# Queries of the first two batches on 128 partitions: a memory-attention and feed-forward kernel with both of its hand-written opening steps listed anew

## The chip, the cores and the metric

The kernel runs on one core of one Trainium2 chip. The metric is the device time of one execution in microseconds (us); three timed runs of the kernel before gave 669.55, 652.33 and 654.77 us, with a median of 654.77 us.

## What is computed

Eight batches of eight heads, 576 tokens and 64 features go through an attention over 32 memory slots, and the result goes through a feed-forward layer of 512 by 2048. All inputs are float32 in memory, except the two weight matrices, which arrive as 64-bit floats.

```python
a = exp(phi - phi.max(axis=2)); a = a / (a.sum(axis=2) + 1e-09)     # per head: 576 tokens x 32 slots
k_m = einsum('bhsm,bhsd->bhmd', a, k); v_m = einsum('bhsm,bhsd->bhmd', a, v)
scores = q @ k_m.T / sqrt(64)
attn = softmax(scores)                                               # over the 32 slots
x = attn @ v_m                                                       # -> 4608 tokens x 512
out = leaky_relu(x @ w_in, 0.01) @ w_out
```

## The kernel before

The kernel never forms `attn @ v_m`: it multiplies the memory values into `w_in` first ("fold"), so that the transposed attention of a batch (8 heads x 32 slots = 256 rows, in two groups g of 128) meets folded weights. Each float32 product of the feed-forward part is made of three float16 products, except that the first 384 tokens run in float32, while the weights are still being read and their bounds are not yet known. The tokens go in groups G: three groups of 384 (batches 0 and 1), then groups of 256.

A batch b goes through steps named `a<b>.<step>`. `phi`, `k`, `v`, `kv` and `q0`, `q1` load; `A` and `B` make the exponentials of phi; `C1` makes the memory keys and values on TensorE, `C2` and `C30` the reciprocal sums, `C3k` scales the keys (tile `x_k`, ScalarE), `C31` the values (`x_v`, VectorE). `D10` transposes `x_k` on TensorE and `D3` copies the result to `kT`; `D11` and `D5` do that for the values (`vT`). `Q0` and `Q1` turn q in 32x32 blocks on VectorE, `E1` multiplies it with `kT` (the scores, in PSUM tiles `psc`), `E2x` turns the scores back to tokens on partitions, into a tile `t1`. A chunk of tokens c then takes `Sc1` (row maximum, VectorE), `Sc2` (subtract; VectorE in chunk 0 of batch 0, else GpSimd), `Sc3` (exp, ScalarE), `Sc4` (row sums, three VectorE instructions), `Sc5` (multiply), `Sc6` (turn back, into tile `a` or a second buffer `t2`), and, outside chunk 0 of batch 0, `Sc7`, `Sc8` (float16 halves on ScalarE and GpSimd).

The weights come in eight quarters `i0` to `i3` and `o0` to `o3`, each in three pieces: `ld` loads 64-bit words to one of eight slots of a buffer `arena`, `y` and `h` prepare the high and low word (`y` on ScalarE; `h` on ScalarE or VectorE), `t` joins them to float32 on VectorE, `b` sums squares on ScalarE. `f0j.1` folds quarter j on TensorE and `f0j.2` copies it from PSUM on ScalarE. `u0.P0` to `u7.O1` are the eight units of the first token group (`P` up-products, `V` the leaky ReLU, `O` down-products). `z.n` puts n products of a tile of ones on TensorE whose result nobody reads. All float32 products run as two passes on TensorE, so `z.3` is six passes in the trace.

The order on every engine is written out by hand: two lists, `OPENING` and `LATER`, name the steps, and each engine runs its own instructions in that order. SyncE issues every load, in the list's order too; it has eight semaphores for them (`DMAHW0` to `DMAHW7` in the rows below), and each load waits until the one eight loads earlier has landed. PSUM is given out by three pools: `ps_a` (3 banks, tiles `pa`), `ps_h` (2, `ph`) and `ps_o` (3, `po`).

In batches 0 and 1, q lies on 96 partitions: partition p holds tokens 6p to 6p+5 of four heads of one parity. A load has 384 runs of 1536 bytes. The 96 partitions make three token blocks tb of 192 tokens, each a row tile of TensorE's array, and a score product is a 32x32 tile with 192 columns; there are 48 of them for each batch, on twelve tiles. `kT` and `x_k` repeat the keys once for each block. Batches 2 to 7 ("far") go another way, which the change leaves as it is.

Of the kernel before, what the change touches and what calls it, by code (L numbers as in the profile page):

```python
# [44 lines left out]
a0.D4 i1.ld0 o0.h1 u0.V0 o0.y1 u1.P0 u1.P1 o0.h2 u1.V0 o0.t2 i1.ld2 a0.S16 o1.ld2 o1.y0 o1.h0 u0.O0  # L45
o1.ld1 u0.P1 a0.S17 i1.y0 o0.t1 u1.V1 i1.h0 i1.h1 i1.y1 i1.t1 u0.V1 i2.ld0 i1.y2 i1.h2 o1.y1 o1.y2
o1.t0 o1.h1 i1.t0 u1.O0 u0.O1 o1.h2 i2.ld1 o2.ld0 i1.t2 f01.1 i2.h0 i2.y0 i2.y1 a0.S18 i2.h1 i2.t1
i2.ld2 f01.2 o2.ld1 o1.t2 o2.ld2 o1.t1 u1.O1 i2.t0 u2.P1 o2.h0 u2.P0 i2.y2 i2.h2 a1.phi o2.y0 i2.t2
o2.t0 a1.kv1 a1.q0 a1.kv0 f02.1 u2.V0 u3.P1 u2.O0 o2.y1 o2.h1 o2.t1 a1.kv2 o2.y2 o2.h2 a1.kv3 a1.A1
u2.V1 u3.P0 o2.t2 i3.ld0 f02.2 a1.q1 a1.A2 a1.A3 u4.P1 a1.B0 u3.V1 u4.P0 a1.B10 u3.V0 i1.b u3.O0  # L50
i2.b u4.V0 a1.B20 u5.P0 a1.B3 o0.b a1.C10 i3.ld2 a1.Q0 i3.ld1 a1.C2 u5.V0 o1.b u2.O1 i3.y0 u5.P1
u4.V1 a1.C30 a1.C31 a1.C3k a1.C4 a1.D10 a1.D2 o2.b i3.h0 a1.D3 a1.Q1 i3.y2 i3.h2 a1.D11 a1.D4 u3.O1
i3.t2 a1.E1 o3.ld0 a1.D5 i3.y1 u4.O0 i3.h1 i3.t0 o3.h0 u5.V1 o3.y0 o3.ld2 u5.O0 a1.E20 i3.t1 a1.E21
i3.b ci.1 o3.ld1 a1.E22 f03.1 a1.S01 a1.S11 a1.S02 a1.S03 a1.S04 u4.O1 o3.y2 o3.y1 o3.h2 ci.2 o3.t0
f03.2 a1.S12 ci.3 ci.4 e. o3.h1 o3.t1 a1.S05 u6.P0 u6.V0 a1.S13 a1.S06 a1.S07 u6.P1 u7.P0 a1.S14
a1.S15 o3.t2 w0.2 u7.V0 u6.O0 a1.S16 o3.b w1.1 co.1 co.2 u7.O0 w1.2 co.3 u6.V1 co.4 u5.O1 o0.k0
a1.S08 o0.k1 o0.k2 u7.P1 e2. o0.l0 u7.V1 o0.l1 u6.O1 a1.S17 a1.S18 o0.l2 u7.O1
# [125 lines left out]
def kernel(  # L183
# [46 lines left out]
    P = 128  # L230
# [6 lines left out]
    KJ = NG * S // P  # L237
    ND = D // 32
# [270 lines left out]
    def attention(b, steps, chunks, f32_chunks=0):  # L509
# [67 lines left out]
        def load_q(g):  # L577
            if far:
                return load_heads(g)
            t = (ld_slot() if b < FB else at(IO * g, IO))[:CP].rearrange(  # L580
                "p (hh j d) -> p hh j d", hh=HP, j=NJ
            )
            nc.sync.dma_start(
                t, q[b].rearrange("(hh g) (p j) d -> g p hh j d", g=NG, j=NJ)[g]
            )
            ld["q", g] = t
# [143 lines left out]
        def _():  # L730
            x_k = att.tile([P, NG, ND, NB, 32], F32, name="x_k")
            if far:
                both = x_k.rearrange("p g db tb x -> p (g db tb x)")
                var["x_k"], var["kS"] = both[:, 0:P], both[:, P:2 * P]
                for g in range(NG):
                    nc.scalar.activation(
                        var["x_k"][:, g * D:(g + 1) * D], var["pk"][g][:, 0:D], AF.Copy,
                        scale=var["r2"][:, 1, g:g + 1],
                    )
                return  # L740
            var["x_k"] = x_k
            for g in range(NG):
                nc.scalar.activation(
                    x_k[:, g],
                    var["pk"][g][:, 0:D].rearrange("p (db o x) -> p db o x", db=ND, o=1)
                    .broadcast_to([P, ND, NB, 32]),
                    AF.Copy, scale=var["r2"][:, 1, g:g + 1],
                )
# [20 lines left out]
        def _():  # L769
# [4 lines left out]
            var["pkT"] = pkT = ps_a.tile([CP, NG, ND, P], F32, name="pa")  # L774
            for g in range(NG):
                for db in range(ND):
                    nc.tensor.transpose(
                        pkT[:, g, db, :],
                        var["x_k"][:, g, db].rearrange("p tb x -> p (tb x)"), ident,
                    )  # L780
# [14 lines left out]
        else:  # L795
            @step("D3")
            def _():
                var["kT"] = kT = att.tile([CP, NG, ND, P], F32, name="kT")
# [31 lines left out]
        def flip_q(g):  # L830
            if far:
# [9 lines left out]
            flat = (  # L841
                (wi[2], wo[1])[g] if b == 0 else ld["ld", 2 + g] if b == 1
                else at((2 * IO, 0)[g], IO)
            )[:CP, 0:HP * NJ * D]
            nc.vector.transpose(flat, ld["q", g].rearrange("p hh j d -> p (hh j d)"))
            var["qT", g] = flat.rearrange(
                "p (hh j db x) -> p hh j db x", hh=HP, j=NJ, db=ND, x=32
# [19 lines left out]
        def scores(gs_):  # L867
            if "psc" not in var:
                shape = [P, E] if far else [P, NG, SB]
                var["psc"] = [ps_a.tile(shape, F32, name="pa") for tb in range(NB)]  # L870
            psc = var["psc"]
            if far:
                if gs_ == (1,):
                    return rows_by(1, 2, 0, JA, JT)
                rows_by(0, 2, 0, JA, JT)
                for j0 in (0, JA // 2):
                    for hh in range(HP):
                        for g in range(NG):
                            rows_by(g, g, j0 * 32, j0, j0 + JA // 2, (hh,))
                return  # L880
            for g in gs_:
                for db in range(ND):
                    for hh in range(HP):
                        for tb in range(NB):
                            rows = slice(tb * 32, (tb + 1) * 32)
                            cols = slice(hh * M, (hh + 1) * M)
                            nc.tensor.matmul(  # L887
                                psc[tb][cols, g, :], var["kT"][rows, g, db, cols],
                                var["qT", g][rows, hh, :, db, :],
                                start=(db == 0), stop=(db == ND - 1),  # L890
                                tile_position=(tb * 32, hh * M),
                            )

        if b == 0:
            steps[f"{name}E10"] = lambda: scores((0,))
        steps[f"{name}E1"] = lambda: scores((1,) if b == 0 else range(NG))
        if far:
            steps[f"{name}E3"] = lambda: scores((1,))

        def flip(tb):  # L900
            if "t1" not in var:
                var["t1"] = att.tile([P, NB, NG * SB], F32, name="t2", bufs=2)
            if far:
                x0, n = ((0, E), (E, E), (2 * E, D), (2 * E + D, D))[tb]
                flat = var["t1"].rearrange("p tb x -> p (tb x)")
                nc.vector.transpose(flat[:, x0:x0 + n], var["psc"][min(tb, 2)][:, 0:n])
                return
            nc.vector.transpose(
                var["t1"][:, tb], var["psc"][tb].rearrange("p g x -> p (g x)")
            )  # L910

        for tb in range(NB + 1 if far else NB):
            steps[f"{name}E2{tb}"] = lambda tb=tb: flip(tb)


        def chunk(c, b0, b1, f32):
            eng = nc.vector if f32 or b >= FB else nc.gpsimd
            shape = [P, (b1 - b0) * NG * SB // M, M]
# [3 lines left out]
            def t1():  # L922
                flat = var["t1"][:, b0:b1].rearrange("p tb x -> p (tb x)")
# [25 lines left out]
            def s6():  # L949
                if "a" not in st:  # L950
                    st["a"] = att.tile([P, 2 * NG * S], F16, name="a", bufs=2)
                if f32:
                    nc.vector.transpose(
                        a_f32(b)[:, b0:b1].rearrange("p tb x -> p (tb x)"), t1()[0]
                    )
                else:
                    own["t2"] = t2 = att.tile([P, (b1 - b0), NG * SB], F32, name="t2", bufs=2)
                    nc.vector.transpose(t2.rearrange("p tb x -> p (tb x)"), t1()[0])

            def places():  # L960

                t2 = own["t2"].rearrange("p tb (g x) -> p tb g x", g=NG)
                if b < FB:
                    a = a_blocks(b)[:, b0:b1]
                    return a[:, :, 0], a[:, :, 1], t2
                flat, a = own["t2"].rearrange("p tb x -> p (tb x)"), a_columns(b)
# [7 lines left out]
            def piece(x, tb):  # L974
                return x[tb] if b >= FB else x[:, tb]

            def s7():
                hi, lo, t2 = places()
                for tb in range(b1 - b0 if b < FB else 2):
                    nc.scalar.copy(piece(hi, tb), piece(t2, tb))  # L980

            def s8():
                hi, lo, t2 = places()
                for tb in range(b1 - b0 if b < FB else 2):
                    nc.gpsimd.tensor_tensor(  # L985
                        piece(lo, tb), piece(t2, tb), piece(hi, tb), ALU.subtract
                    )
# [5 lines left out]
        for c, (b0, b1) in enumerate(chunks):  # L993
            chunk(c, b0, b1, c < f32_chunks)

    def a_f32(b):

# [487 lines left out]
```

## Time and profile before

| | before |
|---|---|
| timed runs, us | 669.55, 652.33, 654.77 (median 654.77) |
| profiled execution, its own time | 655.37 us |
| span of that execution, first to last instruction | 653.4 us |
| TensorE matmul busy | 635.2 us, 97% of the span |
| VectorE, ScalarE, GpSimd busy | 515.4, 392.5, 29.5 us |
| granted TensorE clock, mean | 0.995 |
| first float32 unit of the feed-forward part (`u0.P0`) starts | 32.68 us |

The profile gives, for each engine, when instructions began and what ended the idle time before them. "Chain" means the page's chain of waits: followed back from the last instruction, at each step to what released it. An engine that is busy all the time sets the length of its stage; a gap on another engine costs nothing by itself. The 2 us between the span and the execution's own time lie outside the instructions.

### The profile page before, as it was taken

The numbers are of one execution on the slowest core, as the hardware profiler recorded it, in microseconds if no ns is written. First come the engines' busy times: TensorE is split into PE (matmuls) and PEld (weight loads), VectorE is DVE, ScalarE is ACT, GpSimd is POOL, SyncE is SP. The second block draws the span as 40 slices with busy tenths as digits, with TensorE's granted clock in tenths as the row PEclk, the third lists the DMA queues.
The fourth block names the chain that finished last, engine by engine and source line by source line (L and its number), as shares of the span: only waits on it lengthen the run. The fifth ranks groups of instructions, "written<-read, shape, count | busy, mean of one in ns | idle before, by whom it ended". The sixth has DMA issues, their size and how long they took to land.

```text
span 653.4 us, 17090 instructions
## 1 busy us (share of the span) xinstructions
PE 635.2 (97%) x7256; PEld 476.3 (73%) x7256; DVE 515.4 (79%) x863; ACT 392.5 (60%) x671; POOL 29.5 (5%) x37
## 2 busy tenths in 40 slices
PE   6799999999999999999999999999999999999997
PEld 3344545665545778888888889887888888889883
DVE  5675889998996899899969975889887897575641
ACT  2698868755473656467546565655665566565543
POOL 0010021000001001001000010000010001000000
PEclk9799999999999999999999999999999999999999
DMA  9999722105601753431155011064104110010102
GB/s 237 405 340 332 246 89 85 46 7 104 194 3 25 142 155 56 111 124 35 25 117 158 1 33 43 11 134 146 34 15 80 27 29 22 14 29 6 34 1 50
DMA packets 85309, 61.16 MB, mean 94 GB/s; under 512 B 61936, under 2 KB 68336, under 8 KB 85232
## 3 DMA queue, kind: packets, MB, share of 16 engines
q1 hardware_dynamic: 85136, 59.94, 33.3%
q8 instruction: 57, 0.93, 0.6%
q10 hardware_dynamic: 96, 0.13, 0.1%
q14 instruction: 20, 0.16, 0.1%
HBM read 50.59 MB, written 9.45 MB: 92 GB/s over the span
## 4 chain that ended last, share of the span: by engine, by line
PE 94%; DMA 2%; ACT 2%; SPq 1%; DVE 0%; issue 0%; ACTq 0%
PE po L1297 31%; PE ph L1229 22%; PE po L1186 16%; PE ph L1114 8%; PE ph L1297 5%; PE pa L1020 4%; PE pa L698 3%; DMA arena<-in_moe_w_in_dram 2%; PE po L1331 1%; PE pa L861 1%; PE pa L1387 1%; ACT wi L1245 1%; PE pa L887 0%; PE pa L344 0%; SPq L549 0%
## 5 line engine op out<-in xcount | busy, mean ns | idle before, releaser
L1297 PEld LDWEIGHTS <-arena 128*128 128x128 f16 x2184 | 209.9, 98 | 31.9 <-issue 8.8
L1245 ACT ACTIVATE wi<-ph,g_sc 128x256 f32<-128x256 f32 (+1 forms) x224 | 99.3, 466 | 164.4 <-PE ph L1229 156.9
L1229 PE MATMUL ph<-a,w_mem 128*128 128x256 f16 (+3 forms) x1440 | 145.3, 246 | 2.9 <-ACT wi L1245 2.9
L1229 PEld LDWEIGHTS <-w_mem 128*128 128x128 f16 x1440 | 114.6, 98 | 17.9 <-issue 6.3
L1297 PE MATMUL po<-arena 128*128 128x256 f16 x936 | 122.2, 273 | 0.0
L1297 PE MATMUL po<-wo,arena 128*128 128x256 f16 x936 | 122.1, 273 | 0.0
L1186 PE MATMUL po<-wo,arena 128*128 128x512 f16 (+1 forms) x384 | 110.3, 433 | 0.0
L1274 DVE TENSOR_TENSOR arena<-arena 128x1024 f16<-128x1024 f32 x52 | 63.6, 1223 | 22.4 <-ACT arena L1270 22.4
L1274 DVE TENSOR_TENSOR arena<-wi,arena 128x768 f16<-128x768 f32 (+1 forms) x60 | 54.7, 912 | 10.1 <-ACT arena L1270 10.1
L1266 DVE TENSOR_TENSOR arena<-wi 128x256 f32<-128x256 f32 x104 | 40.4, 430 | 25.6 <-ACT wi L1245 25.1
L1270 ACT CAST arena<-arena 128x1024 f16<-128x1024 f32 x52 | 54.5, 1047 | 8.2 <-DVE arena L1266 8.0
L1114 PE MATMUL ph<-a,w_mem 128*128 128x192 f16 (+2 forms) x304 | 52.2, 317 | 0.7 <-ACT t L936 0.7
L1186 PEld LDWEIGHTS <-arena 128*128 128x128 f16 x288 | 27.9, 98 | 29.7 <-issue 0.6
L1270 ACT CAST arena<-wi 128x768 f16<-128x768 f32 (+1 forms) x60 | 46.6, 777 | 1.5
L1266 DVE TENSOR_TENSOR arena<-wi,arena 128x256 f32<-128x256 f32 x104 | 45.8, 440 | 1.8
L1297 PE MATMUL ph<-wo,arena 128*128 128x256 f16 x312 | 42.6, 273 | 0.0
L985 POOL TENSOR_TENSOR a<-t,a 128x1024 f16<-128x1024 f32 (+2 forms) x16 | 21.9, 1385 | 431.9 <-ACT a L980 431.9
L1186 PEld LDWEIGHTS po<-wo,arena 128*128 128x128 f32 x96 | 17.7, 190 | 20.3 <-issue 18.5
L1020 PE MATMUL pa<-wi,vT 64*32 64x512 f16 (+1 forms) x704 | 28.9, 420 | 0.4 <-ACT vT L805 0.4
L1114 PEld LDWEIGHTS <-w_mem 128*128 128x128 f16 x240 | 20.7, 98 | 10.3 <-issue 4.1
L1053 ACT ACTIVATE w_mem<-pa 128x512 f16<-128x512 f32 x40 | 22.7, 596 | 8.4 <-PE pa L1020 7.4
L1121 ACT ACTIVATE arena<-ph,g_sc 128x384 f32<-128x384 f32 x32 | 18.4, 581 | 15.6 <-PE ph L1114 15.3
(216 smaller groups left out, 750.9 us busy)
## 6 DMA issues: line engine op xcount, KB each, us to landing
out_dram<-obs SPq DMA_DIRECT2D x142, 64.0 KB, 1.7
arena<-in_k_dram SPq DMA_DIRECT2D x28, 288.0 KB, 4.7
arena<-in_v_dram SPq DMA_DIRECT2D x28, 288.0 KB, 4.9
arena<-in_q_dram SPq DMA_DIRECT2D x96, 72.0 KB, 2.8
arena<-in_moe_w_in_dram SPq DMA_DIRECT2D x12, 512.0 KB, 9.5
arena<-in_moe_w_out_dram SPq DMA_DIRECT2D x8, 768.0 KB, 7.3
arena<-in_phi_dram SPq DMA_DIRECT2D x7, 576.0 KB, 5.1
arena<-in_q_dram SPq DMA_DIRECT2D x4, 576.0 KB, 9.3
```

What stands on the lines that cost most here:

```text
L698: nc.tensor.matmul(var["pk"][g][hh * M:(hh + 1) * M, cs], ld["phi"][rows, hh, j, :], ld["kv", hh][rows, kinds[0]:kinds[-1] + 1, j, :], sta ...
L985: nc.gpsimd.tensor_tensor(piece(lo, tb), piece(t2, tb), piece(hi, tb), ALU.subtract)
L1020: nc.tensor.matmul(pf[g][cols, :], lhs, rhs, start=(n == 0), stop=(n == len(passes) - 1), tile_position=(g * D, hh * M),)
L1053: nc.scalar.activation(tiles(halves(w16(b, j), g)[:, 0]), w(g), AF.Copy, scale=ws)
L1114: nc.tensor.matmul(ph[:, t0:t0 + n * SB], lhs, rhs, start=(m == 0), stop=(m == len(seq) - 1))
L1186: nc.tensor.matmul(po, lhs, rhs, start=(f == 0 and m == 0), stop=(f == NQ * NF - 1 and m == len(seq) - 1),)
L1229: nc.tensor.matmul(ph[:, t0:t0 + n], lhs, rhs, start=(m == 0), stop=(m == len(seq) - 1))
L1245: nc.scalar.activation(dst, ph, AF.Prelu, scale=g_sc2[:, j:j + 1], alpha=SLOPE)
L1266: nc.vector.tensor_tensor(gt[:, x], y, z, op)
L1270: nc.scalar.copy(dst[:, 0], src)
L1274: nc.vector.tensor_tensor(dst[:, 1], src, dst[:, 0], ALU.subtract)
L1297: nc.tensor.matmul(acc, g[:, x, s, u], rhs, start=(h == 0 and j == 0 and u == 0 and m == 0), stop=(j == NQ - 1 and u == 1 and m == 2), ski ...
```

## The change

For batches 0 and 1, a load of q covers two head pairs on all 128 partitions: partition p holds nine tokens of each, in 256 runs of 2304 bytes. A 32-partition block r then holds one head parity g and one block of 288 tokens (r = 2g + block). `x_k` and `kT` repeat the keys twice and not three times; `D10` is two transposes of 128x128 and not four of 128x96. The scores of a batch are 32 products with 288 columns on sixteen 32x32 tiles, in four PSUM tiles and not three. Batch 0 takes these four from three pools (`ph`, `po`, `ph`, `pa`) in one step `E1`; batch 1 takes all from `ps_a`, which has three banks, so blocks 0, 2 and 1 are made in `E1` and block 3 in a step `E3` behind one unit's down-products. The turns back (`E2x`) follow the new blocks; batch 0 has six and batch 1 four, against three each. The chunks of batch 0 stay 384 and 192 tokens; those of batch 1 become 288 and 288 (192 and 384 before). The attention tile `a` is addressed by token columns.

The list `OPENING` is written anew, `LATER` is the same. The diff, cut to its core:

```diff
-a0.phi0 a0.A10 z.4 a0.phi1 a0.A11 a0.A2 a0.k a0.A3 a0.B0 a0.q0 a0.B10 a0.B11 a0.B20 a0.q1 a0.B21
-a0.C10 i0.ld0 i0.ld1 a0.B3 a0.C2 i0.ld2 z.1 a0.C30 a0.v a0.C3k a0.D10 a0.Q0 a0.D3 a0.E10 a0.Q1
-a0.E1 i0.y0 i0.h0 o0.ld0 i0.t0 z.3 a0.E21 a0.E20 i0.y1 i0.h1 o0.ld2 a0.S01 o0.ld1 o1.ld0 i0.y2
-i0.h2 i0.t2 a0.C11 a0.S02 i0.t1 a0.S03 i0.b a0.E22 a0.S11 a0.C31 o0.y0 a0.D11 a0.S12 a0.D5 f00.1
-o0.h0 a0.S04 i1.ld1 o0.y2 a0.S05 f00.2 a0.S06 a0.C4 z.1 a0.S13 u0.P0 a0.D2 o0.t0 a0.S14 a0.S15
+a0.phi0 a0.A10 z.3 a0.phi1 a0.A11 a0.A2 a0.k a0.A3 a0.B0 a0.q0 a0.B10 a0.B11 a0.B20 a0.q1 a0.B21
+a0.C10 i0.ld0 i0.ld1 a0.B3 a0.C2 i0.ld2 z.1 a0.C30 a0.v a0.C3k a0.D10 a0.Q0 a0.D3 a0.Q1 a0.E1 i0.y0
+i0.h0 o0.ld0 i0.t0 z.3 i0.y1 i0.h1 o0.ld2 a0.E20 a0.E21 a0.E22 a0.E23 a0.S01 o0.ld1 o1.ld0 i0.y2
+i0.h2 i0.t2 a0.C11 a0.S02 i0.t1 a0.S03 i0.b a0.E24 a0.E25 a0.S11 a0.S04 a0.C31 o0.y0 a0.D11 a0.S12
+a0.D5 f00.1 o0.h0 i1.ld1 a0.S05 f00.2 a0.S06 a0.C4 z.1 a0.S13 u0.P0 a0.D2 o0.t0 a0.S14 a0.S15
...
-            t = (ld_slot() if b < FB else at(IO * g, IO))[:CP].rearrange(
-                "p (hh j d) -> p hh j d", hh=HP, j=NJ
-            )
+            t = ld["q", g] = ld_slot()[:, 0:2 * KJ * D]
             nc.sync.dma_start(
-                t, q[b].rearrange("(hh g) (p j) d -> g p hh j d", g=NG, j=NJ)[g]
-            )
-            ld["q", g] = t
+                t.rearrange("p (hh j d) -> p hh j d", hh=2, j=KJ),
+                q[b].rearrange("h s d -> (h s) d").rearrange(
+                    "(hh gp j) d -> gp hh j d", gp=P, j=KJ
+                )[:, 2 * g:2 * g + 2],
+            )
...
-            x_k = att.tile([P, NG, ND, NB, 32], F32, name="x_k")
+            x_k = att.tile([P, ND, NG, 2, 32], F32, name="x_k")
...
-            var["pkT"] = pkT = ps_a.tile([CP, NG, ND, P], F32, name="pa")
-            for g in range(NG):
-                for db in range(ND):
...
+            var["pkT"] = pkT = ps_a.tile([P, ND, P], F32, name="pa")
+            for db in range(ND):
+                nc.tensor.transpose(
+                    pkT[:, db, :], var["x_k"][:, db].rearrange("p g tb x -> p (g tb x)"), ident
+                )
...
+        def rows_of(rs):
+
+            for r in rs:
+                pool, name, n = (
+                    (ps_h, "ph", GT), (ps_o, "po", E), (ps_h, "ph", GT), (ps_a, "pa", E)
+                )[r] if b == 0 else (ps_a, "pa", E)
+                psc[r] = pool.tile([P, n], F32, name=name)
+            for x in range(2):
+                for db in range(ND):
+                    for hh in (2 * x, 2 * x + 1):
+                        for r in rs:
+                            rows, cols = slice(r * 32, (r + 1) * 32), slice(hh * M, (hh + 1) * M)
                             nc.tensor.matmul(
-                                psc[tb][cols, g, :], var["kT"][rows, g, db, cols],
-                                var["qT", g][rows, hh, :, db, :],
-                                start=(db == 0), stop=(db == ND - 1),
-                                tile_position=(tb * 32, hh * M),
+                                psc[r][cols, 0:HB], var["kT"][rows, db, cols],
+                                var["qT", x][rows, hh % 2, :, db, :], start=(db == 0),
+                                stop=(db == ND - 1), tile_position=(r * 32, hh * M),
                             )
...
+            steps[f"{name}E1"] = lambda: rows_of((0, 2, 1, 3))
+        else:
+            steps[f"{name}E1"] = lambda: rows_of((0, 2, 1))
+            steps[f"{name}E3"] = lambda: rows_of((3,))
...
-            0: (((0, 2), (2, 3)), 1), 1: (((0, 1), (1, 3)),)
-        }.get(b, (((0, NB),),)))
+            0: (((0, GT), (GT, S)), 1), 1: (((0, HB), (HB, S)),)
+        }.get(b, (((0, S),),)))
```

Three places show what this moves. The first is TensorE in batch 0, from the transposed keys to the first product of the values (`pa`, `ph`, `po` are PSUM tiles, `wi_87` and `wo_91` the two turned halves of q, `ones` the products without use, `wi_88` the exponentials of phi and `wo_92` the values; the brackets name the engine or the load that the row waits for). Before:

```order
L777 MATMUL pa<-ident,x_k 96x128
L887 MATMUL pa<-wi_87,kT 32x192 [waits DVE_49,Activation_49]
L887 MATMUL pa<-wi_87,kT 32x192 [waits PE_49] x2
L887 MATMUL pa<-wi_87,kT 32x192 x21
L887 MATMUL pa<-wo_91,kT 32x192 [waits DVE_49]
L887 MATMUL pa<-wo_91,kT 32x192 x23
L1387 MATMUL pa<-ones 128x512 [waits DVE_49]
L1387 MATMUL pa<-ones 128x512 x2
L698 MATMUL po<-wo_92,wi_88 32x64 [waits DMAHW5_49]
```

And now:

```order
L778 MATMUL pa<-ident,x_k 128x128
L876 MATMUL ph<-wi_87,kT 32x288 [waits DVE_49,Activation_49]
...
L876 MATMUL ph<-wo_91,kT 32x288 [waits DVE_49]
...
L876 MATMUL pa<-wo_91,kT 32x288
L1379 MATMUL pa<-ones 128x512 [waits PE_49]
L1379 MATMUL pa<-ones 128x512 x2
L700 MATMUL po<-wo_92,wi_88 32x64 [waits DMAHW5_49]
```

The products of ones (`z.3`) waited for VectorE, which had to turn one score tile back and so free a bank; now only one of the four score tiles is in that pool, and they wait for nothing but TensorE itself.

The second place is VectorE in batch 0, from the second piece of `i0` to the end of chunk 0 (`t` holds the scores, `tm` and `ts` maxima and sums, `x_v` the values, `a` the finished chunk). Before:

```order
L406 SCALAR_TENSOR_TENSOR wi_86<-arena 128x768 [waits DMAHW3_49,DMAHW2_49]
L908 STREAM_TRANSPOSE t_308<-pa 128x384 [waits PE_49]
L928 TENSOR_REDUCE tm<-t_308 128x12 [waits DVE_49]
L754 TENSOR_SCALAR x_v<-po,r_228 128x64 [waits PE_49] x2
L940 TENSOR_REDUCE ts__420<-t_308 128x24 [waits Activation_49]
L941 TENSOR_SCALAR ts__420<-ts__420 128x24 [waits DVE_49]
L942 RECIPROCAL ts__420<-ts__420 128x24 [waits DVE_49]
L945 TENSOR_TENSOR t_308<-t_308,ts__420 128x768 [waits DVE_49]
L953 STREAM_TRANSPOSE a<-t_308 128x768 [waits DVE_49]
```

And now:

```order
L408 SCALAR_TENSOR_TENSOR wi_86<-arena 128x768 [waits DMAHW3_49,DMAHW2_49]
L921 STREAM_TRANSPOSE t_293<-po 128x192
L921 STREAM_TRANSPOSE t_293<-pa 128x192
L942 TENSOR_REDUCE tm<-t_293 128x12 [waits DVE_49]
L954 TENSOR_REDUCE ts__385<-t_293 128x24 [waits Activation_49]
L955 TENSOR_SCALAR ts__385<-ts__385 128x24 [waits DVE_49]
L956 RECIPROCAL ts__385<-ts__385 128x24 [waits DVE_49]
L756 TENSOR_SCALAR x_v<-po,r_227 128x64 [waits PE_49] x2
L959 TENSOR_TENSOR t_293<-t_293,ts__385 128x768 [waits DVE_49]
L967 STREAM_TRANSPOSE a<-t_293 128x768 [waits DVE_49]
```

The three instructions of the row sums (`S04`) stood behind the scaled values (`C31`), which wait for TensorE; now they stand ahead of them. The turn back of the rest became two instructions.

The third place is TensorE in batch 1, around the scores (`po` rows are down-products of the first token group). Before:

```order
L1186 MATMUL po<-wo_92,arena 128x512 x3
L887 MATMUL pa<-arena,kT 32x192 [waits DVE_49,Activation_49]
L887 MATMUL pa<-arena,kT 32x192 [waits PE_49]
L887 MATMUL pa<-arena,kT 32x192 [waits Activation_49]
L887 MATMUL pa<-arena,kT 32x192 x45
L1186 MATMUL po<-wo_93,arena 128x512 x6
```

And now:

```order
L1189 MATMUL po<-wo_92,arena 128x512 x3
L876 MATMUL pa<-arena,kT 32x288 [waits DVE_49,Activation_49]
L876 MATMUL pa<-arena,kT 32x288 [waits DVE_49]
L876 MATMUL pa<-arena,kT 32x288 [waits Activation_49]
L876 MATMUL pa<-arena,kT 32x288 x21
L1189 MATMUL po<-wo_93,arena 128x512 x3
L876 MATMUL pa<-arena,kT 32x288 [waits DVE_49]
L876 MATMUL pa<-arena,kT 32x288 x7
L1189 MATMUL po<-wo_93,arena 128x512 x3
```

The last eight products wait for VectorE to free a bank, with the three down-products of `u4.O0` ahead of them.

More of the change, by code (lines that the diff above doesn't have):

```diff
@@ L46 @@
[L46 to L56, printed above, removed]
@@ new lines @@
+a1.kv3 u3.P0 o2.t2 i3.ld0 a0.S18 f02.2 a1.q1 a1.A2 a1.A3 u4.P1 a1.B0 u3.V1 u4.P0 a1.B10 u3.V0 i1.b
+u3.O0 i2.b u4.V0 a1.B20 u5.P0 a1.B3 o0.b a1.C10 i3.ld2 i3.ld1 a1.C2 u5.V0 o1.b u2.O1 i3.y0 u5.P1
+u4.V1 a1.C30 a1.C31 a1.C3k a1.C4 a1.D10 a1.Q0 a1.D2 o2.b i3.h0 a1.D3 a1.Q1 i3.y2 i3.h2 a1.D11 i3.t0
+a1.D4 u3.O1 i3.t2 o3.ld0 a1.D5 a1.E1 i3.y1 u4.O0 a1.E3 a1.E20 i3.h1 a1.E21 a1.E22 u5.V1 o3.y0
+o3.ld2 i3.t1 i3.b u5.O0 a1.E23 o3.ld1 f03.1 a1.S01 a1.S11 a1.S02 ci.1 a1.S03 o3.h0 a1.S04 u4.O1
+o3.y2 o3.h2 ci.2 o3.t0 f03.2 a1.S12 ci.3 o3.y1 ci.4 e. o3.h1 a1.S05 u6.P0 u6.V0 a1.S13 a1.S06
@@ L58 @@
+a1.S07 o3.t1 u6.P1 u7.P0 a1.S14 a1.S15 o3.t2 w0.2 u7.V0 u6.O0 a1.S16 o3.b w1.1 co.1 co.2 u7.O0 w1.2
+co.3 u6.V1 co.4 u5.O1 o0.k0 a1.S08 o0.k1 o0.k2 u7.P1 e2. o0.l0 u7.V1 o0.l1 u6.O1 a1.S17 a1.S18
+o0.l2 u7.O1
 """
@@ L237 @@
     KJ = NG * S // P
+    HB = S // NG
     ND = D // 32
@@ L917, in chunk @@
+        def chunk(c, x0, x1, f32):
             eng = nc.vector if f32 or b >= FB else nc.gpsimd
-            shape = [P, (b1 - b0) * NG * SB // M, M]
+            w = NG * (x1 - x0)
+            shape = [P, w // M, M]
             n = f"{name}S{c}"
```

199 lines of the change are left out of this document (87 added, 112 removed).

## Prediction

> **What bounds the kernel now.** I read the page's busy times and slices first, then windows, then the chain of waits through the opening.
>
> ```profile
> span 653.4 us, 17090 instructions
> PE 635.2 (97%) x7256; PEld 476.3 (73%) x7256; DVE 515.4 (79%) x863; ACT 392.5 (60%) x671; POOL 29.5 (5%) x37
> PE   6799999999999999999999999999999999999997
> DMA  9999722105601753431155011064104110010102
> ...
> 40.00:60.00 20.00, 20.00 (x80) 8.81 (x78) 13.61 (x18) 16.63 (x27) 0.00 (x0) 1.00 0.99 328
> 60.00:80.00 20.00, 20.00 (x289) 11.18 (x289) 14.36 (x24) 18.55 (x26) 0.00 (x0) 1.00 0.84 276
> 300.00:650.00 350.00, 347.51 (x4175) 298.59 (x4172) 261.63 (x439) 203.57 (x363) 11.59 (x11) 1.00 0.20 48
> ```
>
> TensorE is busy for all of 40 to 80 us and for 347.5 of the last 350 (the first number behind a window's length is PE). So there are two ways to win: let TensorE's unbroken stretch begin earlier, or take work out of it. Loads fill the DMA engines only in the first eight slices or so. The chain shows what the beginning hangs on:
>
> ```profile
> 5.97 12.91 DMA arena<-in_moe_w_in_dram
> 18.96 0.92 ACT arena L397
> 20.68 0.96 DVE wi L406
> 21.64 0.50 DVE t L908
> 22.19 4.84 PE pa L1387 x6
> 27.03 1.63 PE po L698 x102
> 28.66 0.47 DVE x_v L754 x2
> 29.54 0.27 ACT vT L805
> 31.21 0.95 ACT w_mem L1370 x2
> 32.68 1.53 PE ph L1114 x4
> ```
>
> The first piece of `i0` lands at 18.88; ScalarE and VectorE convert it (`y0`, `h0`, `t0`); behind `t0` VectorE turns a score tile back, which frees a bank for the six useless passes of `z.3`; behind those come the values (`C11`), their scaling, the first fold, and at 32.68 `u0.P0`, from which TensorE has no gap to speak of. So the change can win or lose what it moves `u0.P0` by, plus what TensorE's work behind it changes.
>
> **The loads of q.** `v`'s first three loads are held until k's last and the two loads of q have landed, the fourth until the first part of `i0` has, so their issues are the landings:
>
> ```profile
> 9.76 0.33 SPq L549 DMA_DIRECT2D wo<-in_v_dram  x1
> 12.43 0.33 SPq L549 DMA_DIRECT2D wo<-in_v_dram  x1
> 15.63 0.33 SPq L549 DMA_DIRECT2D wo<-in_v_dram  x1
> 16.69 0.33 SPq L549 DMA_DIRECT2D wi<-in_v_dram  x1
> ...
> DMA packets 357, 0.73 MB, mean 364 GB/s; under 512 B 38, under 2 KB 48, under 8 KB 357
> DMA packets 305, 0.45 MB, mean 224 GB/s; under 512 B 13, under 2 KB 305, under 8 KB 305
> DMA packets 242, 0.42 MB, mean 211 GB/s; under 512 B 10, under 2 KB 216, under 8 KB 242
> DMA packets 143, 0.38 MB, mean 192 GB/s; under 512 B 13, under 2 KB 55, under 8 KB 143
> ...
> wi<-in_v_dram SPq DMA_DIRECT2D x1, 288.0 KB, 8.4
> ```
>
> The packet rows are the windows 5 to 7, 9 to 11, 11 to 13 and 13 to 15 us. In the first k passes, in runs of 2304 bytes on 128 partitions: 364 GB/s. In the other three, where q passes, the same busy engines move 1.25 MB in 6 us. The new q has k's shape. At k's rate 1.25 MB take 3.4 us, so everything behind q lands 2.6 us earlier: `i0`'s first piece at 16.3, v's last load (16.69 + 8.4 = 25.1) at 22.5. The bounds are 0, if the slow stretch has another cause, and 2.6; I take 2.6, since k's row is the nearest in every respect.
>
> [...]
>
> **The opening on VectorE.**
>
> ```profile
> 13.80 1.77 DVE L845 STREAM_TRANSPOSE wi<-arena 96x1536 f32<-96x1536 f32 x1
> ...
> 21.56 1.04 DVE L908 STREAM_TRANSPOSE t<-pa 128x384 f32<-128x384 f32 x2
> 26.14 0.58 DVE L908 STREAM_TRANSPOSE t<-pa 128x384 f32<-128x384 f32 x1
> ...
> 28.64 0.48 DVE L754 TENSOR_SCALAR x_v<-po,r 128x64 f32<-128x64 f32 x2 [1.34 <-PE po L698]
> 29.03 0.94 DVE L940 TENSOR_REDUCE ts__420<-t 128x24 f32<-128x768 f32 x1
> ...
> 30.56 0.96 DVE L945 TENSOR_TENSOR t<-t,ts__420 128x768 f32<-128x768 f32 x1
> 31.55 0.98 DVE L953 STREAM_TRANSPOSE a<-t 128x768 f32<-128x768 f32 x1
> ```
>
> `Q0` and `Q1` shrink from 1536 to 1152 columns, some 0.45 us each; `x_k`, `D10`, `D3` and the shorter first `z` also bring the scores forward. None of it is on the path: VectorE still has `t0` ahead of the first turn back, and `t0` waits for `i0`. With `i0` 2.6 us earlier `t0` begins at 18.1. From there to the end of `S06` I keep the row order of before (20.68 to 32.53), with three edits. The four turns of chunk 0 (288, 288, 96, 96 columns) against two of 384: by the rows 0.58 for 384 and 1.77 for 1536 a column costs 1.0 ns and an instruction 0.18, so two more cost 0.2 us net of overlap; the rest in two turns costs 0.1. `S04` ahead of `C31` fills the 1.34 us in which VectorE stood waiting for `C11`. So `S06` ends at 32.53 - 2.6 - 1.34 + 0.3 = 28.9, and `C31`, which stands just ahead of `S05` and `S06` (30.56 to 32.53, 1.97 us), ends at 26.95.
>
> **The new last wait: the fold.** `C31` is now later than its input. `z.3` no longer waits for VectorE and runs right behind the scores, at about 17 to 19.5; `C11` runs when v is there, 22.5 to 24.2, and then waits for nobody. From `C31` the way is `D11`, `D5` (0.67 us from 29.13 to 29.80 before), `f00.1`, `f00.2`, with `z.1` between `f00.1` and `u0.P0` on TensorE:
>
> ```profile
> 29.86 1.09 PE L1020 MATMUL pa<-wi,vT 64*32 64x512 f32 x16 [0.36 <-ACT vT L805]
> ...
> 19.00:19.50 0.50, 0.46 (x30) 0.42 (x34) 0.00 (x0) 0.50 (x1) 0.00 (x0) 0.92 1.00 387
> 26.00:26.50 0.50, 0.50 (x2) 0.10 (x1) 0.50 (x2) 0.48 (x2) 0.00 (x0) 0.76 1.03 422
> 28.00:30.00 2.00, 1.09 (x70) 0.74 (x60) 1.33 (x3) 1.51 (x5) 0.26 (x2) 1.00 1.02 408
> ```
>
> The granted clock (third number from the end) fell to half near 19.46, in a stretch of small score tiles and gaps, and came back near 26.26, 4.1 us after `z.3` began. In the new order TensorE has, from 19.5 to 27.6, only the 1.6 us of `C11`; I take it that the clock is at half when `f00.1` begins at 27.65. Then `f00.1` takes 2.05 us (1.02 doubled), `z.1` 1.6 us (two of `z.3`'s passes of 0.81), and `u0.P0` begins at 31.35, with `f00.2` (29.7 + 1.05) ready ahead of it. Recovery 4.1 us after 27.65 comes at 31.75; 0.4 us of unit work at half clock loses 0.2. In effect `u0.P0` moves from 32.68 to 31.55: a gain of 1.1 us. At full clock all along, `f00.1` would end at 28.7, `f00.2` at 29.8: a gain of 2.9.
>
> [...]
>
> **Batch 1, inside TensorE's unbroken stretch.** Here every TensorE microsecond counts.
>
> ```profile
> 65.82 2.25 PE L698 MATMUL pa<-arena 64*32 64x128 f32 x144
> 75.47 1.93 PE L887 MATMUL pa<-arena,kT 32*32 32x192 f32 x96
> 72.20 0.44 PE pa L777 x4
> ```
>
> `D10` halves: -0.2. The scores are 64 passes of 288 columns in place of 96 of 192, as many columns, but not on sixteen tiles at once: `E1` uses twelve and `E3` four. By columns on each tile: the second row gives 1.86 us (75.47 to 77.33) for 1536, 1.2 ns each, the first 2.2 us for 2304 on eight tiles, 0.95 ns. `E1` and `E3` have 1152 columns a tile each: together 2.2 to 2.8 us, so +0.3 to +0.9. By passes alone it would be 1.24, -0.6. I take +0.6, by the row that it is made of. The GpSimd steps on 576 and 576 columns, and `D4`, `S17`, `S18` in later places, I cost at nothing: TensorE has queued work there. The turns of q for batch 1 save 0.9 us on VectorE and nothing on TensorE. Batch 1: +0.4.
>
> **Sum.** -1.1 + 0.4 = -0.7, so the profiled execution (653.4 of span, 655.37 with what lies around it) becomes 654.7. The median of the runs, 654.77, is 0.6 lower than that execution; the time asked for is such a median, so the forecast is **654.1**.
>
> **The rivals**, all against 654.77.
> - *The clock holds.* `C11` and the light work keep it up, or it is back before `f00.1`: -2.9 + 0.4, so 652.3. For it: between 28 and 30 us before, the granted clock stayed at 1.00 with TensorE busy for 1.09 of 2 us. Against: 8 us with 1.6 us of work.
> - *q is no faster (slower than before).* The slow stretch comes from something that the run length doesn't change, and `i0` still lands at 18.88. Then `S06` ends at 31.5, `C31` at 29.55, `f00.1` runs at half clock from 30.25 to 32.3, `z.1` ends at 33.9, and `u0.P0` begins at 34.0, 0.2 of it lost: +1.5 + 0.4, so 656.7. It decides from a saving of less than 1.9 us on q. For it: the 143 packets of 13 to 15 us kept sixteen engines busy for 2 us, and most are long ones of `i0`. [...]
> - *The clock comes back late.* Half clock for as long as before, 6.8 us from `f00.1`: until 34.45, 1.55 us lost: +0.2 + 0.4, so 655.4.
> - *A stall at `E3`.* It waits for VectorE's first turn back of batch 1. `u4.O0` covers 2.6 us; before, VectorE came to that turn 1.84 us behind the first score. Later than some 1.4 us more, TensorE stands; 2 us of it give 656.
>
> **How the numbers follow.** Forecast 0.42, clock holds 0.23, q no faster 0.17, clock late 0.1, stall 0.08. The range goes from 650.0 (652.3 less the 2.4 by which the lowest run lies under the median) to 657.3 (656.7 and the 0.6 of the profiled execution). No case leaves 2%, which is about what a measurement of this kernel can tell from no change: 0.02, 0.95, 0.03, the outer ones for what I haven't seen.
>
> **What the profile after would show.** Right: the second `v` issue after 9.76 at about 13.0 in place of 15.63, `i0` at 16.3, the six passes of ones ahead of `t0`'s end, half clock at `f00.1`, `u0.P0` near 31.3 with TensorE waiting for itself or ScalarE and no longer for VectorE, and two groups of scores in batch 1 of 1.1 to 1.4 us each. Wrong: packets of q as slow as before, `C11` still waiting for v behind `S04`, or gaps on TensorE between 32 and 110 us.

## The result and the profile after

The changed kernel takes 656.86 us in the median of eight runs (655.48 to 658.42), the kernel before 653.90 in eight (652.18 to 669.55). The ratio, which leaves out the slow execution at 669.55 us, is 1.0056, with a 95% interval from 1.0039 to 1.0072: 2.6 to 4.7 us slower. The forecast was 0.7 us faster. The profiled execution took 657.72 us, against 655.37 before.

The page after gives the span, TensorE's busy time, and q8, the queue whose packets the stalls below follow:

```profile
span 655.8 us, 16957 instructions
PE 636.0 (97%) x7186; PEld 475.6 (73%) x7186; DVE 514.1 (78%) x867; ACT 391.0 (60%) x670; POOL 29.4 (4%) x36
q8 instruction: 56, 0.92, 0.6%
```

TensorE has 70 passes fewer, and yet 0.8 us more busy time and a span 2.4 us longer: there is 1.6 us more idle time, and it has to be found. The opening first, by timelines of SP, ScalarE, VectorE and TensorE (start, length, then the instruction; in brackets the idle time before it and who ended it) and windows:

```profile
9.17 3.26 SPq L551 DMA_DIRECT2D wo<-in_v_dram  x3
13.50 0.33 SPq L551 DMA_DIRECT2D wi<-in_v_dram  x1
14.77 0.94 ACT L399 ACTIVATE arena<-arena 128x768 f32<-128x768 f32 x1
26.21 0.98 DVE L967 STREAM_TRANSPOSE a<-t 128x768 f32<-128x768 f32 x1
25.36 0.33 PE L785 MATMUL pa<-ident,x_v 128*128 128x128 f32 x1 [2.03 <-DVE x_v L756]
26.05 1.76 PE L1027 MATMUL pa<-wi,vT 64*32 64x512 f32 x16 [0.35 <-ACT vT L805]
27.74 2.08 PE L1379 MATMUL pa<-ones 128*128 128x512 f32 x2
29.61 0.56 PE L1119 MATMUL ph<-a,w_mem 128*128 128x384 f32 x1
9.00:11.00 2.00, 1.51 (x110) 1.51 (x114) 1.24 (x3) 0.95 (x2) 0.00 (x0) 0.57 1.06 383
11.00:13.00 2.00, 1.95 (x59) 1.15 (x43) 1.30 (x6) 0.00 (x0) 0.00 (x0) 0.58 0.99 353
28.00:30.00 2.00, 2.00 (x3) 0.84 (x4) 1.39 (x3) 2.00 (x4) 0.00 (x0) 0.56 1.03 402
```

The rate (last number of a window) in the two windows where q passes is 383 and 353 GB/s in place of 224 and 211. The clock (third from the end) is partly at half in both (1.00 before), but VectorE's first turn back still followed `t0` without a wait. `v`'s fourth load is issued at 13.50 (16.69 before), ScalarE has the first piece of `i0` by 14.77 (18.96), `S06` ends at 27.19 (32.53), and `u0.P0` begins at 29.61 in place of 32.68. So the opening gained 3.1 us, though `f00.1` and `z.1` partly ran at half clock (1.76 and 2.08 us; the granted clock from 28 to 30 us is 0.56; by the trace's clock records it was at half from 26.34 to 29.75). Then the lead goes, first in the stretch up to the first FP16 products, which began at 106.76 before:

```profile
49.91 1.55 PE L1189 MATMUL po<-wo,arena 128*128 128x512 f32 x3 [0.58 <-ACT arena L1126]
73.04 1.85 PE L876 MATMUL pa<-arena,kT 32*32 32x288 f32 x48
77.59 1.19 PE L876 MATMUL pa<-arena,kT 32*32 32x288 f32 x16
105.46 0.66 PE L1119 MATMUL ph<-a,w_mem 128*128 128x192 f16 x6
```

A new gap of 0.58 us ahead of `u2.O0`, and 3.0 us for batch 1's scores in place of 1.93. At 105 us 1.3 us are left. The waits on TensorE from 110 to 650 us tell the rest, first of after, then of before (total, times, longest):

```profile
PE pa L700 <- issue: 3.4, 2, 1.8
PE ph L1222 <- ACT wi L1238: 3.3, 6, 0.9
...
PE ph L1229 <- ACT wi L1245: 3.3, 6, 0.9
```

The second row has its twin in the last; the first has none. "issue" means that TensorE waited for nothing that the profile shows. These are the two places:

```profile
204.34 2.37 PE L700 MATMUL pa<-arena 64*32 64x128 f32 x125
208.48 0.62 PE L700 MATMUL pa<-arena 64*32 64x128 f32 x19 [1.77 <-issue]
...
421.38 2.01 PE L700 MATMUL pa<-arena 64*32 64x128 f32 x127
424.98 0.51 PE L700 MATMUL pa<-arena 64*32 64x128 f32 x17 [1.58 <-issue]
```

Both stand inside the kv products (`C10`) of batches 3 and 6, which the change doesn't touch: 144 passes at two instructions each, which take 2.2 to 2.8 us in the other batches. Together: -3.1 + 0.6 + 1.1 + 0.1 (the rest up to 105 us) + 3.35 = about +2.1 us, and the two profiled executions are 2.35 apart. The rest is in the same places: `C10` of batch 3 begins 1.50 us earlier than before (204.34 against 205.84), that of batch 4 0.54 later (249.09 against 248.55), that of batch 6 0.53 later (421.38 against 420.85) and that of batch 7 2.39 later (496.58 against 494.19). So the two stalls cost 2.0 and 1.9 us, somewhat more than their idle rows say.

### The profile page after: what moved, and what is told of

Read it like the earlier page. It is cut to its first block, busy times and chain, and to the rows that moved or that the text cites. A ratio compares the mean times of both kernels' runs of the same rounds, so it can differ in the third digit from the quotient of the medians.

```text
span 655.8 us, 16957 instructions
## 1 busy us (share of the span) xinstructions
PE 636.0 (97%) x7186; PEld 475.6 (73%) x7186; DVE 514.1 (78%) x867; ACT 391.0 (60%) x670; POOL 29.4 (4%) x36
## 4 chain that ended last, share of the span: by engine, by line
PE 94%; DMA 2%; ACT 1%; issue 1%; DVE 1%; SPq 0%; ACTq 0%
PE po L1290 31%; PE ph L1222 22%; PE po L1189 16%; PE ph L1119 8%; PE ph L1290 5%; PE pa L1027 4%; PE pa L700 3%; DMA arena<-in_moe_w_in_dram 2%; PE po L1324 1%; PE pa L858 1%; DMA wo<-in_k_dram 1%; ACT wi L1238 1%; PE pa L876 0%; PE pa L1379 0%; PE pa L346 0%
## 5 line engine op out<-in xcount | busy, mean ns | idle before, releaser
L992 POOL TENSOR_TENSOR a<-t,a 128x1024 f16<-128x1024 f32 (+3 forms) x15 | 21.8, 1467 | 449.2 <-ACT a L988 449.2
```

Source lines behind the costliest of these rows:

```text
L992: nc.gpsimd.tensor_tensor(lo, t2, hi, ALU.subtract)
```

## The experiments

**Theory A.** TensorE's program comes by q8, in 56 packets of 16 KB (0.92 MB): some 258 of its 14460 recorded instructions each. The change took 137 instructions out ahead of batch 2, so all piece boundaries behind it fall on other instructions. A burst of 288 short instructions that begins with a piece uses it up before the next one is there. Rivals: data loads in the way of the fetch, or the new order (B); the split scores (C).

### 34, 16 and 64 small products

```
-i0.h0 o0.ld0 i0.t0 z.3 i0.y1 ...
+i0.h0 o0.ld0 i0.t0 zs i0.y1 ...        # zs: z.3, then n of these:
+    nc.tensor.matmul(pi[0:32, 0, 0:32], ones[0:32, 0:32], ones[0:32, 0:32],
+                     start=True, stop=True, tile_position=(0, 0))
```

> The changed kernel with 34 small products of ones (32x32, FP32, result unused) behind the second z.3 of the opening, where TensorE stands idle from 20.1 to 25.4 us. An FP32 product is two passes, each a weight load and a product, so this puts 136 instructions more into TensorE's stream ahead of everything that follows; of the order, the loads and the other engines nothing changes. The change itself had taken 137 out (by the instructions recorded ahead of the same work, index 9292 before and 9155 after). Theory A (instruction fetch: TensorE's program comes in pieces of 256 instructions, and a burst of short products outruns the fetch where it begins with a piece): the boundaries are back within one instruction of where they stood in the kernel before, both stalls at the kv products (1.77 and 1.58 us) are gone and no new one comes; 656.9 - 3.4 = 653.5 us, the kernel before or a little faster. Theory B (the stalls come from data loads that collide with the fetches, or from the new order of the steps): nothing of that changes, both stalls stay, 656.9 us. Theory C (the loss is that of the split scores of batch 1 and the steps behind them): 656.9 us as well.

> The same with 16 small products, 64 instructions. Theory A: counted on the trace of the changed kernel, the piece boundaries now fall at the beginning of the kv products of batch 5 (near 320 us) and no longer at those of batches 3 and 6: one stall of about 1.7 us in place of two with 3.35, at another batch; 656.9 - 3.35 + 1.7 = 655.2 us. Theories B and C: stalls at batches 3 and 6 as they were, 656.9 us.

> The same with 64 small products, 256 instructions: one whole piece. Theory A: all boundaries fall on the same instructions as in the changed kernel, so both stalls stay at the same products with 1.6 to 1.8 us each; 656.9 us. If the small products as such took the stalls away (by time, heat or clock), they would be gone here as well: 653.5 us. Theories B and C: 656.9 us, so this run is a control of the other two.

Measured: 652.28 us with 34 (ratio to the kernel before 0.9973, 0.9956 to 0.9990), 654.62 with 16 (1.0018, 1.0004 to 1.0032), 663.76 with 64 (1.0145, 1.0121 to 1.0169). With 34 no row "issue" is left behind 28 us. With 16 the only stall there is in batch 5, the place that theory A named, and with 64 one is in batch 6; one row each from the timelines, then from the waits of the run with 64:

```profile
322.02 0.41 PE L700 MATMUL pa<-arena 64*32 64x128 f32 x6 [1.38 <-issue]
...
429.32 0.51 PE L700 MATMUL pa<-arena 64*32 64x128 f32 x17 [1.47 <-issue]
...
PE po L700 <- issue: 2.2, 1, 2.2
```

The run with 64 missed its time by 7 us. Batch 3's stall did not come, so the length of a stall, and near its limit whether there is one, is not fixed by the boundary alone (the packets of q8, below, tell more). And the opening lost 5.6 us (`u0.P0` at 35.20). The small products themselves last 4.94 us and hold `C11` back to 25.22 (20.08 in the changed kernel); a new wait for instructions of 2.2 us appears in `C11` (the last row), where the loads fill the DMA engines (a busy share of 1.02 from 20 to 26 us and 0.97 from 26 to 32); and the clock is at half from 23.44 to 37.10.

The run with 34 gained 1.2 us more than theory A gives. These are its windows and its `u0.P0`, and then a window of the run with 64:

```profile
20.00:26.00 6.00, 4.89 (x222) 4.08 (x229) 5.86 (x13) 4.40 (x6) 0.87 (x2) 1.00 1.02 410
28.00:30.00 2.00, 2.00 (x9) 1.22 (x8) 1.21 (x4) 2.00 (x5) 0.57 (x1) 1.00 1.02 399
27.54 1.45 PE L1119 MATMUL ph<-a,w_mem 128*128 128x384 f32 x4
...
20.00:26.00 6.00, 6.00 (x187) 5.58 (x191) 4.58 (x9) 3.63 (x4) 0.87 (x2) 0.79 1.02 409
```

With 34, TensorE is busy for 4.89 of the 6 us ahead of the fold (2.76 in the changed kernel), the clock (third from the end) is at 1.00 from 28 to 30 us where the changed kernel had 0.56, and `u0.P0` comes 2.1 us earlier. That the busy time of the small products holds the clock is not shown, and the last row speaks against it: with 64, TensorE is busy for all 6 us, and the clock fell at 23.44, while they ran. The 34 products also move `C11` from 20.08 to 22.41 and so shorten the gap ahead of `D11` from 2.03 to 0.75 us. Which of the two kept the clock up stays open.

### The kernel before, shifted

The same with 30 small products in the kernel before, behind its second `z.3`.

> The kernel before with 30 small products behind its second z.3, 120 instructions: 256 less 137 is 119, so the boundaries of the pieces fall where the changed kernel has them, with nothing of the change in it. Theory A: the kernel before gets two stalls of its own, at the kv products of batches 3 and 6, 1.2 to 1.8 us each; 653.9 + 3.0 = 656.9 us (bounds 656.3 to 657.5). Theories B and C: the kernel before has neither the new order nor the split scores, no stall comes, 653.9 us.

Measured: 664.86 us (1.0171, 1.0147 to 1.0196).

```profile
34.04 1.20 PE L1020 MATMUL pa<-wi,vT 64*32 64x512 f32 x10 [2.25 <-issue]
214.75 0.62 PE L698 MATMUL pa<-arena 64*32 64x128 f32 x19 [1.47 <-issue]
430.47 0.59 PE L698 MATMUL pa<-arena 64*32 64x128 f32 x18 [0.86 <-issue]
```

Without any of the change, the kernel before stalls in batches 3 and 6: 2.3 us of the 3.0 expected. The rest is again the opening: of the 8.0 us by which this execution's span is longer than before's, 5.3 are lost ahead of the first FP16 products (112.03 against 106.76), where the fold itself waited 2.25 us for instructions.

The place can be had exactly. I numbered TensorE's recorded instructions (weight loads, products, semaphore steps) by their start, and looked up the first one behind each stall on "issue" that is quoted here. The one of before is this row, in the opening:

```profile
19.05 1.41 PE L887 MATMUL pa<-wo,kT 32*32 32x192 f32 x39 [1.06 <-issue]
```

```
kernel            first instruction behind the stall     less 193, over 256
before            449 (opening scores, 19.05 us)         1
after             3777, 9409                             14, 36
16 products       6849                                   26
64 products       961 (opening), 9665                    3, 37
before, shifted   961 (fold), 4033, 9665                 3, 15, 37
```

All lie on one grid of 256, and so do the stalls of the two runs below that keep the changed kernel's count. B and C have no reason for that.

The packets of q8 in the traces show the rest. At each of these stalls TensorE went on 1.4 to 1.5 us after the end of a packet: in the changed kernel the packets ran from 205.89 to 207.09 and from 422.37 to 423.58, and TensorE went on 1.39 and 1.40 us behind them. So it is the fetch that TensorE waits for; A is shown. But 256 short instructions are not enough for a stall. In the kernel before, 256 instructions of batch 2's `C10` ran up to a boundary at 144.6 in 1.80 us, and no stall followed: the last packet before the boundary had begun 0.5 us ahead of the first of them. In the run with 64, batch 3's had begun 0.7 us ahead. At the changed kernel's two stalls it began 1.6 and 1.2 us after the first of the 256. What sets when a packet begins is not shown.

### The burst cut in two

```
-        steps[f"{name}C10"] = lambda: slots_of((0, 1))
+        steps[f"{name}C10"] = lambda: slots_of((0, 1), range(4) if far else range(KJ))
+        steps[f"{name}C1+"] = lambda: slots_of((0, 1), range(4, KJ))
```

In the list `LATER`, a product step stands between the two parts.

> The changed kernel without any added product; only, in batches 2 to 7 the kv products of C10 (72 FP32 products, 288 instructions in 2.0 us) are issued as 32 and 40, with the next product step of the list between them (in batch 3 O22.0, nine products, 1.95 us; in batch 6 d24.1, six products, 0.65 us). Theory A (a burst outruns the fetch of the next 256 instructions): the time that lies in between is taken off the stall, so batch 3's 1.77 us goes, batch 6's 1.58 us falls to about 0.9; 656.9 - 1.8 - 0.7 = 654.4 us. Theory B (the stalls come from data loads that run at those times): the products still run in the same microseconds, both stalls stay, 656.9 us.

Measured: 667.3 us. In batch 6 the second part stood behind the load of q, which takes kv's place: it read q in place of kv, and TensorE waited 7.8 us for that load. So the time says nothing; in batch 3 no stall was left.

> The changed kernel without added products, the kv products of C10 in batches 2 to 7 issued as 32 and 40 with a product step between them, as in the run split; but in batch 6 the first part now stands ahead of d24.0 and the second behind it, both ahead of the load of q that takes kv's place, so that nothing of the computation changes. Theory A (a burst outruns the fetch of the next 256 instructions): batch 3's 1.77 us goes, batch 6's 1.58 us falls to 0.9 or goes, since d24.0 (six products, 0.65 us) now lies inside the burst; 656.9 - 1.8 - 0.7 to 1.6 = 653.5 to 654.4 us. Theory B (the stalls come from data loads at those times): both stay, 656.9 us. Against the run with 34 small products (652.3) what is left is the second thing those did, holding TensorE's clock at the first fold: some 1.2 us.

Measured: 658.23 us (1.0079, 1.0053 to 1.0105). Batches 3 and 6:

```profile
206.31 1.78 PE L701 MATMUL pa<-arena 64*32 64x128 f32 x64
208.03 2.12 PE L1191 MATMUL po<-wo,arena 128*128 128x512 f16 x9
210.07 1.37 PE L701 MATMUL pa<-arena 64*32 64x128 f32 x80
...
427.95 0.51 PE L701 MATMUL pa<-arena 64*32 64x128 f32 x17 [0.92 <-issue]
```

The stalls did what theory A said: batch 3's is gone, batch 6's is 0.92. The time did not. The two parts of batch 3 take 3.15 us, against 2.72 in one piece with 34 small products (202.34 us there), and those of batches 2, 4, 5 and 7 take 0 to 0.4 us more. Two waits that the changed kernel does not have stand at 229.74 (0.33 us, for VectorE) and 338.78 (0.72 us, for ScalarE). And this execution, the longest of its six, had a late opening, with `u0.P0` at 30.48. The opening has the same code in the changed kernel (29.61) and in the run before this one (28.55), so one trace gives `u0.P0` to about a microsecond. How much of this is in the median stays open.

### The place of z.3

```
-... i0.t0 z.3 i0.y1 ... a0.C11 a0.S02 ...
+... i0.t0 i0.y1 ... a0.C11 z.3 a0.S02 ...
```

> The changed kernel with the second z.3 (three products of ones, 2.8 us) behind the value products C11 in place of ahead of them; TensorE's instructions are as many as in the changed kernel ahead of everything behind D11, so by theory A both stalls (1.77 and 1.58 us) stay where they are. [...]

Measured: 656.46 us (1.0051, 1.0032 to 1.0069), no gain that can be told from the changed kernel's 1.0056.

```profile
24.38 2.46 PE L1379 MATMUL pa<-ones 128*128 128x512 f32 x5
26.67 0.27 PE L785 MATMUL pa<-ident,x_v 128*128 128x128 f32 x1
27.30 1.09 PE L1027 MATMUL pa<-wi,vT 64*32 64x512 f32 x16 [0.36 <-ACT vT L805]
29.29 1.13 PE L1119 MATMUL ph<-a,w_mem 128*128 128x384 f32 x3
```

`f00.1` ran at full clock, 1.09 us in place of 1.76 (the clock was at half from 21.26 to 24.68 here; why it fell there is not shown), but `D11` now stood behind `z.3` and came 1.3 us later. The two nearly cancel. The stalls stayed at 3777 and 9409, shorter this time (0.91 and 1.31 us).

### Batch 1's scores in one group, and u2.O0 put back

```
-            steps[f"{name}E1"] = lambda: rows_of((0, 2, 1))
-            steps[f"{name}E3"] = lambda: rows_of((3,))
+            steps[f"{name}E1"] = lambda: rows_of((0, 2, 1, 3))      # tile 3: ps_h, "ph"
```

> The changed kernel with the 34 small products, and batch 1's four score tiles in one group as in batch 0 (the fourth tile in a ph bank), in place of E1 with three and E3 with one. Theory 1 (the loss in batch 1 comes from having only twelve and then four of the sixteen tiles at work): the scores take 1.9 us in one group (batch 0's second half with all four took some 0.9) in place of 1.78 + 1.12, and with TensorE busy behind it this reaches the end: 652.3 - 1.0 = 651.3 us. Theory 2 (the columns set it, and how they are grouped doesn't matter): 652.3 us. If the ph bank comes free too late, TensorE waits at E1 and the time is above 652.3 us.

Measured: 651.71 us (0.9966, 0.9953 to 0.9979), the lowest of all. Its scores run from 71.50 to 73.4 us, 1.9 in one group in place of 3.0, as theory 1 has it. In this trace the first FP16 products begin 0.6 us earlier than with 34 products alone (103.69 against 104.30), though `u0.P0` came 0.6 later (28.14 against 27.54), within the spread of the opening. The medians are 0.6 apart too, but the intervals of the two ratios overlap: the gain stands in the trace and is not shown in the time.

> The changed kernel with the 34 small products, and u2.O0 behind f02.1 as the kernel before has it, in place of right behind u2.P0 and u2.V0. Expected: the new gap of 0.58 us in which TensorE waits for ScalarE's leaky step (49.9 us in the changed kernel) is gone; 652.3 - 0.6 = 651.7 us. If the time is made good elsewhere, or f02.1 waits for its own inputs in that place: 652.3 us.

Measured: 654.24 us (1.0008, 0.9999 to 1.0017), 2 us slower than without. The gap of 0.58 us went, and this came:

```profile
50.23 1.05 PE L1027 MATMUL pa<-wi,vT 64*32 64x512 f32 x4 [1.40 <-DVE wi L408]
```

`f02.1` stood at that place before VectorE had its weights; `u2.O0` had covered that wait. The four passes behind the wait take 1.05 us by themselves; in the run with 34 products all sixteen take 1.09. So the 0.58 is the price of a better order, not a fault of it.

### Why q is faster

Both with 34 small products; q's loads in two DMAs, by rows or by partitions.

> The changed kernel with the 34 small products, and each of q's loads of batches 0 and 1 in two DMAs, of four and of five of the nine rows: runs of 1024 and 1280 bytes on the same 128 partitions, shorter than the 1536 bytes of the kernel before. Theory P (the new load is faster because it lies on 128 partitions in place of 96): q moves at 350 GB/s or more as before the split, i0 lands as early, 652.3 us and up to 0.3 more for the two further issues. Theory R (it is faster because of its longer runs): q falls to some 200 GB/s, everything behind it in the opening comes 2.5 to 3 us later, and 654.5 to 655.3 us.

> The changed kernel with the 34 small products, and each of q's loads of batches 0 and 1 in two DMAs, one for partitions 0 to 95 and one for 96 to 127, with the runs of 2304 bytes as they are. [...] Theory L (what slowed q in the kernel before was its layout as a whole, rows of 1536 bytes from far apart, and not the partitions of a DMA): the two DMAs fill each other's gaps, 350 GB/s or more, 652.3 us.

Measured: 652.49 us by rows (0.9986, 0.9973 to 0.9999), 655.55 by partitions (1.0026, 1.0007 to 1.0046). The windows 9 to 11 and 11 to 13 us, by rows, then by partitions:

```profile
9.00:11.00 2.00, 1.49 (x109) 1.49 (x113) 1.24 (x3) 0.98 (x2) 0.00 (x0) 0.60 1.07 371
11.00:13.00 2.00, 1.94 (x61) 1.18 (x45) 1.30 (x6) 0.00 (x0) 0.00 (x0) 0.55 1.04 389
...
9.00:11.00 2.00, 1.60 (x117) 1.60 (x121) 1.24 (x3) 0.87 (x2) 0.00 (x0) 0.50 1.02 225
11.00:13.00 2.00, 1.95 (x53) 1.07 (x37) 1.26 (x7) 0.00 (x0) 0.00 (x0) 0.50 1.08 239
```

Runs of 1024 and 1280 bytes cost nothing that shows (371 and 389 GB/s). Loads that lie on 96 and on 32 partitions fall to 225 and 239 GB/s, near the 224 and 211 of the kernel before and not the 350 or more of theory L, with `v`'s fourth issue at 15.24 and `u0.P0` at 30.91. Both runs have two DMAs for each load, so their number is not the cause. The gain comes from all 128 partitions in one DMA, as theory P has it, and not from the run length. Why a load on fewer partitions is slower is not shown.

## Why the prediction was wrong

- **What failed: "plus what TensorE's work behind it changes", priced by batch 1 alone.** The prediction took TensorE's unbroken stretch to move with `u0.P0`, and of gaps on TensorE it listed under wrong only those "between 32 and 110 us". Two stalls of 1.77 and 1.58 us at 207 and 423 us, in steps with unchanged code, turned the sign: TensorE waited there for its own instructions. It counted the passes that the change removes by the time they take, never by where their absence puts the rest of the program. A sign of it was in the trace of before: at 19.05 us a score product stands with 1.06 us on "issue", at number 449 of the grid. It was off the path and I passed over it.
- **The loads of q: right in direction, too small.** 2.6 us foreseen; `v`'s fourth issue came 3.2 earlier and the first piece of `i0` at least 4.1. The rate was right (364 taken from k's row, 353 to 383 where q passes); the slow stretch was taken too short. Before, the four windows from 7 to 15 us moved 267, 224, 211 and 192 GB/s, 1.79 MB together, and the prediction left out the first. After, they moved 361, 383, 353 and 416; at their mean of 378, 1.79 MB take 4.7 us in place of 8, an estimate of 3.3 us earlier. The reason is the 128 partitions, as the two loads of q show; the runs of 2304 bytes, named beside them, have no part in it that shows.
- **The opening on VectorE** ended at 27.19 (28.9 foreseen), which follows from the earlier `i0`.
- **The new last wait: the fold.** The half clock at `f00.1` was there, from 26.34 us, a little after its start, and lasted 3.4 us (4.1 foreseen). `u0.P0` at 29.61 in place of 31.35: this term gave -3.1 and not -1.1. The path behind it was right: from `f00.1` to `u0.P0` 3.56 us passed (3.70 foreseen). The difference is that `f00.1` began at 26.05 in place of 27.65, which follows from the earlier loads. The clock costs about what the prediction said: at full clock, in the run with 34 small products, `u0.P0` came at 27.54, 2.1 earlier (1.8 foreseen), with the opening's spread of about a microsecond in it. The rival *the clock holds* is what that run made, by other means.
- **Batch 1: right in mechanism, undersized.** Scores +1.1 for +0.6, since the price was taken from columns on each tile; with twelve and with four of sixteen tiles at work the array is the less filled, and one group of sixteen takes 1.9. The 0.58 us at 49.9, which I had cost at nothing, came from an order that avoids a larger wait.
- **The stall at `E3`** did not come, and q was not "no faster".
- **The DMA row** was misread: its slices show the engines at 7 tenths or more in the first five, not "the first eight slices or so". No term hangs on it.

So -0.7 would have been -1.5 by the start of batch 3's `C10`, and the two stalls made it +2.4 at that of batch 7's. The measured 656.86 us lies inside the range that was given, and beside the 656.7 of *q is no faster*. That is luck: q was faster, and no case had the fetch.

## What to carry to other kernels

Before trusting a small gain in a kernel that TensorE bounds, look for rows "issue" inside bursts of small products, and number the instructions: if the stalls lie on one grid, then an edit that changes the count ahead of them can move them, for better or worse (here 137 instructions fewer brought two stalls of 1.77 and 1.58 us, and 136 more took them away), and a gain under 1% may be that alone. Compare a layout change at an equal instruction count, or at several. A few cheap instructions in an idle place can move the grid, as 34 products did here (-5.4 us by the ratios 1.0056 and 0.9973, the higher clock at the fold included), but 64 in the same place cost more than they gave (1.0145): they held `C11` up by 5.1 us, and a boundary of the grid fell into it, with a wait of 2.2 us.

## What the runs showed of the hardware

- TensorE's stalls on "issue" that are quoted here lie on a grid of 256 recorded instructions, and in the changed kernel q8 brought some 258 of these with a packet. A stall at a boundary took 0.9 to 2.3 us in the rows quoted here and ended 1.4 to 1.5 us after a packet of q8. In `C10` it hit where the 256 ahead of the boundary ran in about 2 us and the last packet began after the first of them; where the packet had begun 0.5 us ahead of the first, 256 in 1.80 us passed without a stall. In the opening it hit a plain fold (2.25 us, the kernel before with 30 small products) and value products (2.2 us, the run with 64, with 380 GB/s of loads from 26 to 32 us) too.
- A load of q on 96 of 128 partitions moved 211 to 224 GB/s, one cut into 96 and 32 partitions 225 to 239, and one on 128 moved 353 to 389, at any run length tried from 1024 to 2304 bytes. The windows hold some other packets as well.
- 34 small FP32 products on one 32x32 tile, 68 passes, took 2.3 us, 34 ns a pass, while `C10`'s passes on eight tiles take some 16 (2.01 us for 127). With 64 such products TensorE was busy for all of 20 to 26 us, and the granted clock fell to half at 23.44 (0.79 over these 6 us).
- Cutting a burst of 144 small passes into 64 and 80 around FP16 products cost 0.4 us in batch 3, by one trace of each kernel.
